# Mixed-head attention and two feed-forward blocks: the head mix ahead of the softmax as three float32r matmuls on rows split two steps ahead

## Chip, cores and metric

One core of a Trainium2 chip runs the whole program. The metric is the device time of one execution in microseconds; the kernel before has a median of 704.97 us over 3 runs (704.95 to 705.08).

## The reference, cut to what matters

```python
# q, k, v: (2, 12, 448, 64);  w_pre, w_post: (12, 12);  float32 throughout
scores = scale * (q @ k^T)                       # per batch and head, 448 x 448
scores = einsum('bhij,hg->bgij', scores, w_pre)  # mix of the heads ahead of the softmax
scores = scores - max(scores, axis=-1)
attn   = exp(scores)
attn   = attn / (sum(attn, axis=-1) + 1e-9)
attn   = einsum('bhij,hg->bgij', attn, w_post)   # mix of the heads behind it
x      = (attn @ v), heads side by side          # 896 x 768
x      = moe(x)    # h = x @ w_in (768 x 2048); h * clip(h + 3, 0, 6) / 6; @ w_out
out    = moe2(x)   # h = x @ w_in; max(h, 0) + alpha * min(h, 0); @ w_out
```

## The kernel before

**Tiles and groups.** The query rows of each batch are cut into tiles of 120 rows (120, 120, 120, 88), eight tiles in all. For each tile and head, TensorE (PE) computes the scores (`qk`, line 197), and ScalarE copies them from PSUM into a tile `S` that has one query row per partition (line 597). The mix runs over heads, so heads must lie on partitions: a DMA (`pull`, line 208) takes 10 query rows of all 12 heads, 120 partition rows of 448 numbers, into a tile `pull`. Such a unit is a group; there are 90 groups.

**Steps.** One loop over `s_` writes the order of the work out by hand; a step is one turn of it. Step `s_` mixes group `s_` with a block-diagonal 120x120 weight (`premix`, line 224: PE in float32, which the trace shows as two matmul records per group), and VectorE takes the negated row maximum (line 226). ScalarE computes the exponential with row sums (`exp`, line 234). In the next step `norm` adds 1e-9 to the sums, inverts them (lines 215, 216), and scales a copy `wr` of the post-mix weights by them (line 218), all on VectorE. Three steps behind `premix`, `post` (line 244) multiplies the exponentials with `wr` in float32 on PE (eight records), and ScalarE evicts the result into `MT` (line 257).

**Around it.** In the same step PE computes the scores of a coming tile, mostly one head (two float32r matmuls with query halves split into a rounded part and its rest); the queries' split is on GpSimd (POOL, lines 169 and 170). In steps 22 to 33 the keys of the second batch are split, one head per step: a cast on VectorE (line 153) and a subtraction on GpSimd (line 154). When all groups of a tile are post-mixed, `av` (line 281) multiplies `MT` with the values: six head pairs per tile, in two bursts of three pairs, half a tile's steps apart; VectorE copies the sums to `xT` (line 294). In steps 57 to 77 the first three weight blocks of the feed-forward part are loaded and converted from 64-bit storage (lines 346 to 369; ScalarE, VectorE, GpSimd in successive steps). From step 77 on there are no more scores to compute; `xT` is split (`split_x`, lines 441 and 442) and the blocks too (lines 374 and 380), and from step 84 on the first feed-forward matmuls (line 446) run between the groups. The feed-forward part that follows, from about 249 us on, is almost PE alone: three float32r matmuls per product (`mm3`).

**Queues and buffers.** Every engine works through its instructions in order. All DMAs are issued by SP. PSUM holds two buffers for the mixed scores (`mx`), two for the scores, two for `post`, two for `av`. `pull` runs four steps ahead and has six buffers.

Of the kernel before, what the change touches and what calls it, by code (L numbers as in the profile page):

```python
# [7 lines left out]
F32 = mybir.dt.float32  # L8
R = mybir.dt.float32r
# [4 lines left out]
ALU = mybir.AluOpType  # L14
# [2 lines left out]

LAG = 3
PL = 4
EB = 384  # L20

W_MIN = 2.0 ** -15
# [13 lines left out]
def kernel(  # L36
# [15 lines left out]
    nc = tc.nc  # L52
    _, D, H, S = k.shape
# [6 lines left out]
    GP = G * H  # L60
# [3 lines left out]
    tiles = []  # L64
    groups = []
    for b in range(B):
        for i0 in range(0, S, GP):
            n = min(GP, S - i0)
            t = len(tiles)
# [7 lines left out]
    NTILE, NG = len(tiles), len(groups)  # L77
# [9 lines left out]
    def pool(stack, name, **kw):  # L87
        return stack.enter_context(tc.tile_pool(name=name, reuse_waits="tile", **kw))
# [5 lines left out]
    late = pool(p_late, "late", bufs=3)  # L94
# [6 lines left out]
    with tc.manual_schedule():  # L101
# [5 lines left out]
        xT = xtp.tile([128, KD, NT], F32, name="xT")  # L107
# [94 lines left out]
        d_t, mx_t, e_t, sm_t, wr_t, pt_t = {}, {}, {}, {}, {}, {}  # L202

        def pull(g):
            ti, o, st, xn = groups[g]
            t = late.tile([GP, S], F32, tag="pull", bufs=PL + 2, name="pull")
            src = S_t[ti][bass.ds(o, xn, step=st)] if st > 1 else S_t[ti][o:o + xn]
# [4 lines left out]
        def norm(g):  # L212
            pm = groups[g][3] * H
            sm = sm_t.pop(g)[:pm]
            nc.vector.tensor_scalar(sm, sm, 1e-9, None, ALU.add)  # L215
            nc.vector.reciprocal(sm, sm)
            wr = wr_t[g] = late.tile([GP, GP], F32, tag="wr", bufs=LAG + 1, name="wr")
            nc.vector.tensor_scalar(wr[:pm], wpost[:pm], sm, None, ALU.mult)

        def premix(g):  # L220
            pn = groups[g][3] * H
            d = d_t.pop(g)
            m = psA.tile([GP, 512], F32, tag="mx", bufs=2, name="mx")
            nc.tensor.matmul(m[:pn, :S], wpre[:pn, :pn], d[:pn], start=True, stop=True)  # L224
            nm = late.tile([GP, 1], F32, tag="nm", name="nm")
            nc.vector.tensor_reduce(nm[:pn], m[:pn, :S], axis=AX.X, op=ALU.max, negate=True)  # L226
            mx_t[g] = (m, nm)
# [69 lines left out]
        qk_at, av_at = {}, {}  # L297
        for ti in range(1, NTILE):
            lo, hi = tiles[ti - 1]["s"] - PL, tiles[ti]["s"] - PL
            first = range(HC) if ti == 1 else ()  # L300
            for h in first:
                qk_at[lo + 1 + h] = [(ti, h)]
            for s_, hs in spread(list(range(len(first), H)), lo + (PL if first else 0), hi).items():
                qk_at.setdefault(s_, []).extend((ti, h) for h in hs)
        k_first = {
            tiles[ti - 2]["s"] - PL - 2: tiles[ti]["b"] for ti in range(tps, NTILE, tps)
        }
        for ti in range(NTILE - 1):
            lo = tiles[ti]["s"] + tiles[ti]["ng"] + LAG
            for z in range(2):  # L310
                av_at[lo + 2 + z * (tiles[ti + 1]["ng"] // 2)] = [(ti, 3 * z + a) for a in range(3)]


        P = {}
# [56 lines left out]
        def conv_hi(i):  # L371
            if i < len(blocks):
                hi = P["w"].tile([128, WC], R, tag="whi", bufs=3, name="whi")
                nc.scalar.copy(hi, b_t[i])  # L374
                w_t[i] = [hi]

        def conv_lo(i):
            if i < len(blocks):
                lo = P["w"].tile([128, WC], R, tag="wlo", bufs=3, name="wlo")
                nc.gpsimd.tensor_tensor(lo, b_t.pop(i), w_t[i][0].bitcast(F32), ALU.subtract)  # L380
                m = KD if blocks[i][0] == "in" else 2
                w_t[i] = [x.rearrange("p (k f) -> p k f", k=m) for x in (w_t[i][0], lo)]
# [56 lines left out]
        def split_x(kk, c, a, z, src, eng):  # L439
            h, l = x_pair(kk, c)  # L440
            nc.scalar.copy(h[:, a:z], src)
            eng.tensor_tensor(l[:, a:z], src, h[:, a:z].bitcast(F32), ALU.subtract)
# [83 lines left out]
            nc.sync.dma_start(out=wmix[nm], in_=src)  # L526
        load_q(1, 0)
        wpre = wmix["pre"]

        wpost = late.tile([GP, GP], F32, tag="wpost", bufs=1, name="wpost")  # L530
        for j in range(H // 2):
# [6 lines left out]
        nc.gpsimd.tensor_copy(  # L538
            wpost.rearrange("p (g x) -> p x g", g=H), wmix["post"].rearrange("p (x g) -> p x g", g=H)
        )  # L540
        for s_ in range(-PL, 6 - PL):
            for (ti, h) in qk_at.get(s_, []):
                if h % HC == 0 and h:
                    load_q(ti, h // HC)

        X = tiles[-1]["s"] - PL
        also = {}

        def at(s_, *fs):
            also.setdefault(s_, []).extend(fs)  # L550

        a = tiles[-3]["s"]
        for i in range(NC):
            at(a, lambda i=i: load_w(i))
            for z, f in enumerate((conv_magnitude, conv_shift, conv_sign, conv_round)):
                at(a + 3 + z, lambda f=f, i=i: f(i))
            a += 7
        at(X, open_early)
        at(X + 1, lambda: nc.sync.dma_start(out=alpha_sb, in_=alpha.rearrange("(k p) -> p k", p=128)))
        for kk in range(KD):  # L560
            at(X + 1 + kk, lambda kk=kk: split_x(kk, 0, 0, S, xT[:, kk, :S], nc.gpsimd))
        for i in range(NC):
            at(X + 2 + 3 * i, lambda i=i: conv_hi(i), lambda i=i: conv_lo(i))
        at(X + 7, lambda: load_w(3), lambda: load_w(4))
        at(NG, lambda: conv_a(3))
        at(NG + 1, lambda: conv_round(3))
# [7 lines left out]
        for s_ in range(-PL, NG + LAG):  # L574
            for g in range(PL) if s_ == -PL else [s_ + PL] if 0 <= s_ < NG - PL else []:
                pull(g)
            for c in range(2) if s_ in k_first else ():
                load_k(k_first[s_], c)
            for ti in range(tps, NTILE, tps):
                if s_ == tiles[ti]["s"] + tiles[ti]["ng"] + LAG:  # L580
                    for c in range(4):
                        load_v(tiles[ti]["b"], c)
            if 0 <= s_ < 4:
                load_v(0, s_)
            if s_ in range(NG):
                premix(s_)
            kk = s_ - (NG - KD)
            if kk == 0:
                p0 = ptile()[:, :S]
            if 0 <= kk < KD:  # L590
                in_part(p0, 0, x_t, 0, kk, kk + 1)
            heads = qk_at.get(s_, [])
            pend = [qk(ti, h, s_ < 0 and h % 2) for (ti, h) in heads]
            if s_ in range(NG):
                exp(s_)
            for z, (d, p) in enumerate(pend):
                (nc.vector.tensor_copy if s_ < -1 and z == 1 else nc.scalar.copy)(d, p)
            for (ti, h) in qk_at.get(s_ + 6, []):
                if h % HC == 0:
                    load_q(ti, h // HC)  # L600
            for (ti, h) in qk_at.get(s_ + 2, []):
                if h % HC == 0:
                    split_q(ti, h // HC)
            for (ti, h) in qk_at.get(s_ - 2, []):
                if ti % tps == tps - 1 and ti + 1 < NTILE:
                    split_k(tiles[ti + 1]["b"], h)
                    if h in (2, 5):
                        load_k(tiles[ti + 1]["b"], h // HC + 2)
            if s_ - 1 in range(NG):
                norm(s_ - 1)  # L610
            if s_ - LAG in range(NG):
                post(s_ - LAG)
                post_evac(s_ - LAG)
            if s_ == NG:
                p1 = in_chain(1, x_t, 0)
                gs[0, 0] = g_tile(0, 0)
                run(act1(p0, gs[0, 0], 0))
            if s_ == NG + 1:
                p2 = ptile()[:, :S]
                in_part(p2, 2, x_t, 0, 0, KD // 2)  # L620
            if s_ == NG + 2:
                in_part(p2, 2, x_t, 0, KD // 2, KD)
                gs[1, 0] = g_tile(1, 0)
                run(act1(p1, gs[1, 0], 1))
            for (ti, h) in av_at.get(s_, []):
                av(ti, h)
            for f in also.get(s_, []):
                f()
# [26 lines left out]
        def out_layer(i, gs, done):  # L655
            for e in range(DM // EB):
                accs = [ptile()[:, :S] for _ in range(2 * EB // 128)]
                for f2 in range(KF // 2):
# [8 lines left out]
                    wt = w_t.pop(i)  # L667
                    for ee in range(EB // 128):
                        for c in range(B):
# [6 lines left out]
                            if last:  # L676
                                done(e * (EB // 128) + ee, c, p)
                    i += 1
# [28 lines left out]
def _laid_out(q, k, v, w_pre, w_post, moe_w_in, moe_w_out, moe2_w_in, moe2_w_out, moe2_alpha):  # L707
# [26 lines left out]
    def w_out(w):  # L734
        f, m = w.shape
        w = w.view(_np.int64).reshape(f // 256, 2, 128, m // EB, EB)
        return w.transpose(3, 0, 2, 1, 4).reshape(-1, 128, 2 * EB)

# [36 lines left out]
```

## Time and profile before

| | |
|---|---|
| median of 3 runs | 704.97 us |
| the profiled execution | 705.02 us, its span 703.0 us, mean granted TensorE clock 0.995 |
| PE busy | 691.4 us (98%) |
| VectorE (DVE) busy | 440.5 us (63%) |
| ScalarE (ACT) busy | 372.5 us (53%) |
| GpSimd (POOL) busy | 324.4 us (46%) |
| chain that ended last | PE 89%, of it line 446 58%, line 244 11%, line 224 10%, line 281 6%, line 197 5% |

A page is of one profiled execution. Busy is the union of an engine's instructions; successive instructions of one engine can overlap by some hundredths to tenths of a microsecond, so what an instruction takes of its queue is the distance between starts. The chain of waits follows the work that ended last back to what released it.

### The profile page before, as it was taken

The numbers are of one execution on the slowest core, as the hardware profiler recorded it, in microseconds if no ns is written. First come the engines' busy times: TensorE is split into PE (matmuls) and PEld (weight loads), VectorE is DVE, ScalarE is ACT, GpSimd is POOL, SyncE is SP. The second block draws the span as 40 slices with busy tenths as digits, with TensorE's granted clock in tenths as the row PEclk, the third lists the DMA queues.
The fourth block names the chain that finished last, engine by engine and source line by source line (L and its number), as shares of the span: only waits on it lengthen the run. The fifth ranks groups of instructions, "written<-read, shape, count | busy, mean of one in ns | idle before, by whom it ended". The sixth has DMA issues, their size and how long they took to land.

```text
span 703.0 us, 11160 instructions
## 1 busy us (share of the span) xinstructions
PE 691.4 (98%) x4164; PEld 610.0 (87%) x4164; DVE 440.5 (63%) x778; ACT 372.5 (53%) x692; POOL 324.4 (46%) x224
## 2 busy tenths in 40 slices
PE   5999999999999999999999999999999999999998
PEld 2677778877788899999999999999999999999997
DVE  5565874456666458888874454348999999535311
ACT  4686566667776656656554443343444454444300
POOL 6331651212226235454567555544455455775630
PEclk9899999999999999999999999999999999999999
DMA  4755554346446022323334423322223322445302
GB/s 154 225 176 181 160 137 124 108 153 190 153 105 163 1 91 90 130 96 102 123 101 154 139 99 105 122 90 86 94 91 113 113 90 95 148 158 182 124 1 78
DMA packets 31874, 85.20 MB, mean 121 GB/s; under 512 B 5966, under 2 KB 21966, under 8 KB 31822
## 3 DMA queue, kind: packets, MB, share of 16 engines
q1 hardware_dynamic: 31822, 84.50, 37.2%
q8 instruction: 33, 0.54, 0.3%
q14 instruction: 19, 0.16, 0.1%
HBM read 62.47 MB, written 2.75 MB: 93 GB/s over the span
## 4 chain that ended last, share of the span: by engine, by line
PE 89%; POOL 6%; issue 3%; DMA 0%; SPq 0%; DVE 0%; POOLq 0%
PE p L446 58%; PE pt L244 11%; PE mx L224 10%; PE av L281 6%; PE sc L197 5%; POOL wb L369 2%; POOL wlo L380 2%; POOL kT L160 1%; DMA kst<-in_k_dram 0%; SPq L127 0%; POOL qT L170 0%; POOL qT L169 0%; POOL wmix_pre L536 0%; POOL wpost L538 0%; DVE o L694 0%
## 5 line engine op out<-in xcount | busy, mean ns | idle before, releaser
L380 POOL TENSOR_TENSOR wlo<-wb,whi 128x768 fp32r<-128x768 f32 x64 | 126.4, 1974 | 127.3 <-ACT whi L374 127.3
L369 POOL TENSOR_TENSOR wb<-wb,wst 128x768 int32<-128x768 int32 x64 | 125.5, 1962 | 101.3 <-DVE wb L362 79.0
L446 PE MATMUL p<-xh,whi 128*128 128x448 f32 x384 | 141.7, 369 | 0.0
L446 PE MATMUL p<-gl,whi 128*128 128x448 f32 x384 | 139.4, 363 | 0.0
L446 PE MATMUL p<-xl,whi 128*128 128x448 f32 x384 | 139.4, 363 | 0.0
L446 PE MATMUL p<-gh,whi 128*128 128x448 f32 x384 | 139.2, 362 | 0.0
L446 PE MATMUL p<-gh,wlo 128*128 128x448 f32 x384 | 138.4, 360 | 0.1
L446 PE MATMUL p<-xh,wlo 128*128 128x448 f32 x384 | 138.3, 360 | 0.0
L354 DVE TENSOR_SCALAR wb<-wb 128x768 f32<-128x768 f32 x64 | 52.6, 822 | 81.6 <-ACT wb L346 81.5
L346 ACT ACTIVATE wb<-wst 128x768 f32<-128x768 f32 x64 | 57.8, 904 | 68.9 <-DMA wst<-in_w_out_dram 50.1
L244 PEld LDWEIGHTS pt<-wr,e 120*112 120x112 f32 x720 | 86.8, 176 | 7.4 <-issue 2.3
L234 ACT ACTIVATE e<-mx,nm 120x448 f32<-120x448 f32 (+1 forms) x90 | 57.2, 635 | 63.2 <-DVE sm L215 46.5
L244 PE MATMUL pt<-wr,e 120*112 120x120 f32 x720 | 88.5, 266 | 0.0
L224 PE MATMUL mx<-pull,wmix_pre 120*120 120x448 f32 x180 | 85.7, 559 | 2.3 <-DMA pull<-S 2.3
L226 DVE TENSOR_REDUCE nm<-mx 120x1 f32<-120x448 f32 (+1 forms) x90 | 55.9, 621 | 45.1 <-PE mx L224 45.0
L374 ACT CAST whi<-wb 128x768 fp32r<-128x768 f32 x64 | 53.2, 832 | 50.6 <-PE p L446 32.4
L446 PEld LDWEIGHTS p<-xh,whi 128*128 128x128 f32 x384 | 72.1, 188 | 6.8 <-issue 1.2
L446 PEld LDWEIGHTS p<-gh,whi 128*128 128x128 f32 x384 | 72.1, 188 | 5.7
L446 PEld LDWEIGHTS p<-gh,wlo 128*128 128x128 f32 x384 | 71.8, 187 | 5.6 <-POOL wlo L380 0.5
L446 PEld LDWEIGHTS p<-xh,wlo 128*128 128x128 f32 x384 | 71.8, 187 | 5.1
L446 PEld LDWEIGHTS p<-xl,whi 128*128 128x128 f32 x384 | 72.1, 188 | 4.7 <-issue 0.9
L197 PE MATMUL sc<-kT,qT 128*120 128x448 f32 (+1 forms) x168 | 75.3, 535 | 0.4 <-POOL qT L170 0.3
(52 smaller groups left out, 896.7 us busy)
## 6 DMA issues: line engine op xcount, KB each, us to landing
wst<-in_w_in_dram SPq DMA_DIRECT2D x32, 768.0 KB
wst<-in_w_out_dram SPq DMA_DIRECT2D x32, 768.0 KB
pull<-S SPq DMA_DIRECT2D x88, 210.0 KB
qst<-in_q_dram SPq DMA_DIRECT2D x20, 180.0 KB
kst<-in_k_dram SPq DMA_DIRECT2D x5, 672.0 KB
v<-in_v_dram SPq DMA_DIRECT2D x8, 336.0 KB
out_dram<-o SPq DMA_DIRECT2D x12, 224.0 KB
qst<-in_q_dram SPq DMA_DIRECT2D x8, 132.0 KB
```

What stands on the lines that cost most here:

```text
L197: nc.tensor.matmul(p[:n, :S], t[:, o, a:a + n], kT[h], start=(o == 0), stop=(o == 1))
L224: nc.tensor.matmul(m[:pn, :S], wpre[:pn, :pn], d[:pn], start=True, stop=True)
L226: nc.vector.tensor_reduce(nm[:pn], m[:pn, :S], axis=AX.X, op=ALU.max, negate=True)
L234: nc.scalar.activation(out=e[:pn], in_=m[:pn, :S], func=ACTF.Exp, bias=nm[:pn], accum_out=sm[:pn])
L244: nc.tensor.matmul(p[:, c * GP:(c + 1) * GP], e[:pn, c * JP:(c + 1) * JP], wr[:pn], start=True, stop=True,)
L281: nc.tensor.matmul(p[64 * o:64 * o + 64, a % 3, :n], v_t[T["b"], h // HC][:, h % HC, c, :], MT[ti][:, c, h, :n], start=(c == 0), stop=(c = ...
L346: nc.scalar.activation(t, s[:, :, 1].bitcast(F32), ACTF.Abs)
L354: nc.vector.tensor_scalar(t, t, W_MAX, W_MIN, ALU.min, ALU.max)
L369: nc.gpsimd.tensor_tensor(n, n, st_t.pop(i)[:, :, 0].bitcast(I32), ALU.add)
L374: nc.scalar.copy(hi, b_t[i])
L380: nc.gpsimd.tensor_tensor(lo, b_t.pop(i), w_t[i][0].bitcast(F32), ALU.subtract)
L446: nc.tensor.matmul(p, wt[a], xt[c], start=(first and z == 0), stop=(last and z == 2))
```

## The change

Groups 0 and 1 are mixed as before. For every later group, two steps ahead of the mix, the pulled rows are rounded to float32r (`sh`; on ScalarE for odd groups, on VectorE for even ones, with some exceptions near the weight conversion), and VectorE subtracts the rounded rows from the pulled ones in place. The mixing weights are split in the same way once. The mix is then three matmuls: rounded weights with rounded rows, rounded weights with the rest, rest of the weights with rounded rows.

`norm` moves from behind the score work to right behind the maximum, and its scaling goes to GpSimd, except in steps with a weight conversion on GpSimd. All six pairs of `av` come in one burst per tile. The second batch's value loads are spread over four steps, and a few splits of activations and weights change their steps.

```diff
+RAW = 2
@@ norm
-            nc.vector.tensor_scalar(wr[:pm], wpost[:pm], sm, None, ALU.mult)
+            if g in by_vector:
+                nc.vector.tensor_scalar(wr[:pm], wpost[:pm], sm, None, ALU.mult)
+            else:
+                nc.gpsimd.tensor_scalar(wr[:pm], wpost[:pm], sm, 1.0, ALU.mult, ALU.mult)
+
+        def split_s(g):
+            if RAW <= g < NG:
+                pn = groups[g][3] * H
+                d = d_t.pop(g)
+                t = late.tile([GP, S], R, tag="sh", bufs=2, name="sh")
+                (nc.scalar.copy if g in by_scalar else nc.vector.tensor_copy)(t[:pn], d[:pn])
+                r = d.bitcast(R)
+                nc.vector.tensor_tensor(r[:pn], d[:pn], t[:pn].bitcast(F32), ALU.subtract)
+                d_t[g] = (t, r)
@@ premix
-            nc.tensor.matmul(m[:pn, :S], wpre[:pn, :pn], d[:pn], start=True, stop=True)
+            if g < RAW:
+                nc.tensor.matmul(m[:pn, :S], wpre[:pn, :pn], d[:pn], start=True, stop=True)
+            else:
+                for z, (a, x) in enumerate(((0, 0), (0, 1), (1, 0))):
+                    nc.tensor.matmul(
+                        m[:pn, :S], wpre_r[a][:pn, :pn], d[x][:pn], start=(z == 0), stop=(z == 2)
+                    )
@@ value bursts
-            for z in range(2):
-                av_at[lo + 2 + z * (tiles[ti + 1]["ng"] // 2)] = [(ti, 3 * z + a) for a in range(3)]
+            av_at[lo + 2] = [(ti, a) for a in range(H // 2)]
@@ start
+        wpre_r = [late.tile([GP, GP], R, tag=f"wpre{z}", bufs=1, name=f"wpre{z}") for z in "hl"]
...
+        nc.gpsimd.tensor_scalar(wpre_r[0], wpre, 1.0, 1.0, ALU.mult, ALU.mult)
+        nc.gpsimd.tensor_tensor(wpre_r[1], wpre, wpre_r[0].bitcast(F32), ALU.subtract)
@@ who does what in the steps with a weight conversion (a = 57, 64, 71)
+        by_vector = set()
+        by_scalar = set(range(1, NG, 2))
...
+            by_vector |= {a + 6, a + 7}
+            by_scalar -= {a + 5}
+            by_scalar |= {a + 7}
@@ splits of activations and weights
-            at(X + 1 + kk, lambda kk=kk: split_x(kk, 0, 0, S, xT[:, kk, :S], nc.gpsimd))
+            at(X + 1 + kk + (kk > 1), lambda kk=kk: split_x(kk, 0, 0, S, xT[:, kk, :S], nc.gpsimd))
-            at(X + 2 + 3 * i, lambda i=i: conv_hi(i), lambda i=i: conv_lo(i))
+            at(X + (3, 8, 10)[i], lambda i=i: conv_hi(i), lambda i=i: conv_lo(i))
@@ the loop over steps
-                if s_ == tiles[ti]["s"] + tiles[ti]["ng"] + LAG:
-                    for c in range(4):
+                if tiles[ti]["s"] + LAG + 4 <= s_ < tiles[ti]["s"] + LAG + 8:
+                    for c in (s_ - tiles[ti]["s"] - LAG - 4,):
                         load_v(tiles[ti]["b"], c)
...
             if s_ in range(NG):
                 premix(s_)
+            if s_ - 1 in range(NG):
+                norm(s_ - 1)
+            if s_ in range(NG):
+                split_s(s_ + 2)
...
-            if s_ - 1 in range(NG):
-                norm(s_ - 1)
             if s_ - LAG in range(NG):
                 post(s_ - LAG)
```

## Rows read from the trace of the kernel before

**Rows 1.** Busy time of each engine, its share of the span, instructions.

```profile
PE 691.4 (98%) x4164; PEld 610.0 (87%) x4164; DVE 440.5 (63%) x778; ACT 372.5 (53%) x692; POOL 324.4 (46%) x224
```

**Rows 2.** Chain of waits in order of time: start us, us, what.

```profile
146.74 0.75 PE mx L224 x2
147.49 0.41 PE sc L197 x2
147.90 0.82 PE pt L244 x8
...
196.13 2.61 PE av L281 x48
198.75 0.94 PE mx L224 x2
...
240.72 1.81 PE p L446 x9
```

**Rows 3.** Timeline of ScalarE: start, us, engine, line, operation, out<-in [idle before].

```profile
144.28 0.63 ACT L234 ACTIVATE e<-mx,nm 120x448 f32<-120x448 f32 x1 [0.37 <-DVE sm L215]
...
144.90 0.52 ACT L597 COPY S<-sc 120x448 f32<-120x448 f32 x1
145.31 0.59 ACT L257 COPY MT<-pt 112x480 f32<-112x480 f32 x1
```

**Rows 4.** Timeline of VectorE, the same step.

```profile
143.56 0.62 DVE L226 TENSOR_REDUCE nm<-mx 120x1 f32<-120x448 f32 x1 [0.79 <-PE mx L224]
144.10 0.14 DVE L215 TENSOR_SCALAR sm<-sm 120x1 f32<-120x1 f32 x1
144.28 0.17 DVE L216 RECIPROCAL sm<-sm 120x1 f32<-120x1 f32 x1
144.48 0.28 DVE L218 TENSOR_SCALAR wr<-wpost,sm 120x120 f32<-120x120 f32 x1
```

**Rows 5.** Lines 153 and 488: duration ns min/median/max, first and last start us.

```profile
L153 DVE CAST kT<-kst x12: 376/377/926, 66.8 to 94.7; 128x448 fp32r<-128x448 f32 x12
...
L488 DVE TENSOR_TENSOR gl<-t,gh x32: 612/618/1920, 474.7 to 593.6; 128x448 fp32r<-128x448 f32 x32
```

**Rows 6.** Groups by form: count, busy us, mean ns of one, idle before.

```profile
L154 POOL TENSOR_TENSOR kT<-kst,kT 64x448 fp32r<-64x448 f32 x12 | 13.7, 1139 | 22.5 <-DVE sm L215 19.9 <-PE pt L244 2.1 <-issue 0.4
L169 POOL TENSOR_SCALAR qT<-qst 128x360 fp32r<-128x360 f32 x19 | 9.7, 511 | 60.5 <-DMA qst<-in_q_dram 48.0 <-PE sc L197 10.1 <-PE pt L244 2.2
L442 POOL TENSOR_TENSOR xl<-xT,xh 128x448 fp32r<-128x448 f32 x6 | 6.8, 1140 | 4.6 <-ACT xh L441 4.6
L170 POOL TENSOR_TENSOR qT<-qst,qT 128x264 fp32r<-128x264 f32 x8 | 6.2, 773 | 0.7
L441 ACT CAST xh<-xT 128x448 fp32r<-128x448 f32 x6 | 3.5, 582 | 0.0
L536 POOL TENSOR_SCALAR wmix_pre<-wmix_pre 120x120 f32<-120x120 f32 x1 | 0.7, 725 | 0.1
```

**Rows 7.** Timeline of VectorE around step 87.

```profile
222.85 1.59 DVE L218 TENSOR_SCALAR wr<-wpost,sm 120x120 f32<-120x120 f32 x1
```

**Rows 8.** Timeline of GpSimd, the same stretch.

```profile
222.55 1.82 POOL L380 TENSOR_TENSOR wlo<-wb,whi 128x768 fp32r<-128x768 f32 x1 [1.66 <-ACT whi L374]
```

**Rows 9.** Stretches: us, busy PE, PEld, DVE, ACT, POOL, clock, DMA share, GB/s.

```profile
65.34:95.41 30.07, 30.07 (x244) 23.30 (x243) 25.66 (x61) 19.82 (x50) 18.05 (x19) 1.00 0.50 160
162.63:200.75 38.12, 38.12 (x326) 30.20 (x325) 24.12 (x70) 28.46 (x67) 7.11 (x8) 1.00 0.49 160
202.74:220.97 18.23, 18.23 (x146) 14.35 (x145) 14.32 (x40) 15.18 (x37) 12.14 (x9) 1.00 0.59 125
```

**Rows 10.** Timeline at the start of the steps, PE.

```profile
17.05 1.48 PE L224 MATMUL mx<-pull,wmix_pre 120*120 120x448 f32 x2 [2.31 <-DMA pull<-S]
...
18.62 0.28 PEld L197 LDWEIGHTS sc<-kT,qT 128*120 128x120 f32 x1 [1.31 <-POOL qT L169]
```

## The prediction

> **What bounds the kernel now.** I read the page's busy shares first, then the chain of waits in order of time, then single steps on the timeline. PE is busy 691.4 of 703.0 us [rows 1]. In the chain a step of the attention stage is PE alone, end to end: mixing pair 0.75 us, two score matmuls 0.41, eight post matmuls 0.82, sum 1.98, and the next step begins where it ends [rows 2]. So what PE sheds is gained, as long as the others deliver in that time. ScalarE has 0.37 us left per step: the score copy starts 0.62 behind the exponential, the eviction 0.41 behind the copy and takes 0.59, of which some 0.1 overlaps what follows: 1.5 together [rows 3]. VectorE uses about 1.1: maximum, the add and the reciprocal take the queue 0.54, 0.18 and 0.20, so 0.92, then the scaling of the post weights [rows 4]. The change spends these reserves.
>
> **PE.** Nine float32r matmuls of 448 columns took 1.81 us on the chain [rows 2], 0.20 each, three 0.60. Against 0.75 that is 0.15 us per group, and 88 of the 90 groups change: 13.2 us. A step would take 1.83. The first mixing pair behind a value burst took 0.94 instead of 0.75 [rows 2]; 14 half bursts become 7 whole ones, 7 x 0.19 = 1.3 us. If nothing else moved, 705.0 - 14.5 = 690.5.
>
> **What VectorE pays.** Every group adds a subtraction with two SBUF inputs: 0.62 us, 0.54 of the queue (as for the maximum, which overlaps its successor by 0.08). Even groups add a rounding copy, 0.38 by the nearest row [rows 5]; odd ones give it to ScalarE, 0.58 by the nearest row [rows 6], about 0.47 of its queue, so 0.24 per step on the mean: 1.74 of 1.83. The scaling of the weights leaves VectorE for GpSimd. Its price there: a tensor_scalar of 360 columns took 0.51, the one of the same 120x120 shape 0.73 beside a working VectorE [rows 6]; between a third of the first (0.17) and 0.73, I take 0.27, since 0.73 holds a wait.
> The two engines stand in each other's way here: while GpSimd's 1.82 us subtraction ran from 222.55 on, a VectorE tensor_scalar that takes 0.28 [rows 4] took 1.59 [rows 7] and ended when that did [rows 8]. The copy ranged from 0.38 to 0.93 and the two-input subtraction from 0.61 to 1.92 [rows 5]. Reductions from PSUM show no such stretch.
> So in a regular step, from maximum to maximum: odd 0.92 + 0.54 = 1.46; even 0.92 + 0.38 + 0.04 (dependent start) + 0.25 (the weights' scaling slips in on GpSimd between copy and subtraction) + 0.54 = 2.13; mean 1.80. A query split on GpSimd (0.51 + 0.77 us, some every third step [rows 6]) can hold VectorE between 0 and 0.4 per step; it mostly runs beside the maximum, so I take 0.1: 1.9 against PE's 1.83. The whole burst of 5.2 us per tile (twice 2.61 [rows 2]) lets VectorE catch up the 0.8 that it falls behind in 12 steps. So 55 regular steps (10 to 21, 34 to 76) keep their saving: 55 x 0.15 = 8.3 us.
>
> **Where the reserve is gone.** Four places.
> - Steps 59 to 75, with the early weight conversion: VectorE was busy 24.12 of 38.12 us [rows 9], 1.42 per step. Plus 0.54, plus half a copy 0.17, minus the scaling 0.20, plus 0.15 of waiting: 2.08 x 17 = 35.4, against PE's new 35.6. No slack, and the conversion comes in lumps: I charge 1.5 us (bounds 0 and 2.6, their whole saving).
> - Steps 22 to 33 split the next batch's keys: per step a VectorE cast and a GpSimd subtraction of 1.14 us [rows 6]; these steps took 30.07 us with two half bursts [rows 9]. The GpSimd subtraction starts some 0.15 behind the cast and holds VectorE's next copy or subtraction until 1.29, though the statistics are done at 0.84. Odd: 1.29 + 0.48 + 0.25 (scaling on GpSimd) + 0.26 (cast) = 2.3. Even: 1.29 + 0.26 + 0.25 + 0.48 + 0.30 = 2.6. Four query splits add 1.2 each, 0.4 per step: 2.85 x 12 = 34.2 us; 1.3 of this is carried out as VectorE's lag into steps with a little reserve: 32.9, so 2.8 us are lost against before (bounds: 1.8 gained if the engines interleave, 6 lost if all waits add).
> - Steps 77 to 85 have no score matmuls, PE 1.57 before; 18.23 us with a half burst [rows 9], 15.4 without. GpSimd has six activation subtractions of 1.14 [rows 6], three weight passes of 1.82 [rows 8] and seven scalings: 14.2 us; VectorE's copies, subtractions and two scalings hold the same path for 9 x 0.54 + 4 x 0.30 + 2 x 0.2 = 6.5. One after the other 20.7, so 5.3 more; the burst at step 86 hides two VectorE steps of lag, 3.3: 2.0 lost (bounds: 1.3 gained, 5 lost). Steps 86 to 89 gain 4 x 0.15 = 0.6.
> - The start: GpSimd splits the mixing weights ahead of a query split for which PE waited 1.31 us [rows 10]: two operations on 120 columns, 0.5 to 1.5 us. Against it stand the 8 x 0.15 = 1.2 of steps 2 to 9. I take zero for both (bounds 0.7 gained, 1.5 lost).
>
> The moves cost nothing by themselves. Adding and inverting the sums behind the maximum delays no exponential (ScalarE already waits for the maximum alone); the value loads are spread over four steps, before the burst that reads them, so SP's pulls wait less. The split waits for a pull two steps earlier than the mixing did; behind a waiting copy on ScalarE stands that step's exponential, behind VectorE's subtraction the next maximum. One pull held PE, the first, for 2.31 us [rows 10]; later ones never did. Taken at nothing, upper bound in the rivals.
>
> **Sum.** 8.3 - 1.5 - 2.8 - 2.0 + 0.6 + 1.3 + 0 = 3.9 us. The profiled execution took 705.02 (span 703.0 and 2.0 around it), the median 704.97, so they are one number here: 705.0 - 3.9 = 701.1 us.
>
> **Rivals.**
> 1. PE stays the only bound: VectorE and GpSimd interleave, buffers carry the lag. For it: VectorE's idle time of 0.79 us per step before its maximum [rows 4] and the bursts. Against it: 2.1 us in an even step. Time: 690.5 plus about 1 at the start, 691.5.
> 2. Slower: the path that VectorE and GpSimd share becomes the step. Place: the copy or subtraction behind the reciprocal. Price: the scaling (0.27) in odd steps too and 0.3 of query split per step: (1.46 + 0.27 + 2.13) / 2 + 0.3 = 2.2 us; less the burst's help, two steps' lag, some 0.2 per step: 2.0, PE's old step. The regular saving of 8.3 is then nil, the losses stay: 705.0 + 1.5 + 2.8 + 2.0 - 1.3 = 710.0 us. It decides from 1.98 us from maximum to maximum on. The stretched scaling of 1.59 us speaks for it, the long quiet stretches of GpSimd against it (7.11 of 38.12 us busy [rows 9]). The Trainium skill ("Perfetto Trace Analysis", section Optimizing Scalar/DVE Operations) speaks against the change in this sense: the two engines share an SBUF read port, so that moving work between them might not help. By that rule the scaling on GpSimd frees nothing, which is this rival's 710; the stretched 1.59 us [rows 7] agrees that one waits for the other.
> 3. Pulls land too late for the earlier split. At seven tile starts the pulls wait for the last score copy; half a us to a us each, 3.5 in sum: 701.1 + 3.5 = 704.6, no change. For it the 2.31 us at the start; against it that no other pull was waited for.
> 4. The three matmuls don't cost less than the pair (0.25 each, 0.75 in all): then 710.0 as well. Against it the score pair, two float32r matmuls in 0.41.
>
> **Chances.** Forecast 0.45, with a range of its own of 698 to 704; rival 1 0.20; rival 2 0.20; rival 3 0.12; rival 4 0.03. The range of 692 to 708.5 leaves out the fast half of rival 1 and the worse half of rivals 2 and 4. A measurement of this kernel tells about 0.2%, 1.4 us, from no change. Faster than 703.6: 0.42 of the forecast, all of rival 1, a little of rival 3: 0.63. Within: 0.11. Slower than 706.4: rivals 2 and 4 and what is worse of 3: 0.26.
>
> **What would show it.** The timeline of PE: three mixing matmuls 0.20 apart and a step of 1.83 us around 145 us; if they are 0.25 apart, rival 4. VectorE's distance from maximum to maximum, odd against even: 1.5 and 2.1, below 1.83 on the mean; from 1.98, rival 2. Steps 22 to 33 and 77 to 85: their windows longer than before, with PE idle ahead of the mixing matmuls; if they are shorter, rival 1. Waits of ScalarE's or VectorE's split for a pull: rival 3. One burst of 5.2 us per tile. The feed-forward stage behind about 249 us must keep its length to 0.5 us; if it doesn't, the reasoning left something out. Wrong altogether: a gain above 14.5 us, or a loss in the regular steps.

## The result and the profile after

The changed kernel takes 715.0 us (713.76 to 716.19, 4 runs) against 705.03, ratio 1.0142, 95% interval 1.013 to 1.0154: 10 us slower, where 701.1 was forecast. Its profiled execution took 714.41 us, span 712.6.

Busy shares and the chain by line, from the page of the changed kernel; the first line answers to [rows 1]:

```profile
PE 686.7 (96%) x4252; PEld 625.5 (88%) x4252; DVE 486.5 (68%) x825; ACT 392.2 (55%) x737; POOL 378.7 (53%) x310
...
PE 75%; DVE 8%; POOL 7%; issue 4%; DMA 4%; ACT 1%; SPq 0%; POOLq 0%; ACTq 0%
PE p L465 57%; PE av L301 5%; PE pt L264 5%; PE mx L242 4%; DMA pull<-S 4%; DVE pull L231 3%; PE sc L198 3%; POOL wb L388 2%; DVE nm L246 2%; POOL wlo L399 2%; POOL kT L161 1%; DVE sh L229 1%; DVE kT L154 1%; DMA kst<-in_k_dram 0%; ACT e L254 0%
```

PE is busy 4.7 us less and yet ends 10 us later: the chain, 89% PE before, now has only 75% on PE and leads over VectorE (8%) and over DMA (4%, the pulls) too. The PE part did what it should. Chain of waits in order of time, a regular stretch (start us, us, what), against [rows 2]:

```profile
127.59 0.61 PE mx L242 x3
128.21 0.41 PE sc L198 x2
128.62 0.82 PE pt L264 x8
129.44 0.61 PE mx L242 x3
```

Three mixing matmuls take 0.61 us instead of 0.75, and the step is 1.85 instead of 1.98. VectorE keeps up there (timeline of VectorE, an odd step, against [rows 4], and the next two maxima):

```profile
130.09 0.62 DVE L246 TENSOR_REDUCE nm<-mx 120x1 f32<-120x448 f32 x1
130.63 0.14 DVE L216 TENSOR_SCALAR sm<-sm 96x1 f32<-96x1 f32 x1
130.80 0.16 DVE L217 RECIPROCAL sm<-sm 96x1 f32<-96x1 f32 x1
131.06 0.63 DVE L231 TENSOR_TENSOR pull<-pull,sh 120x448 fp32r<-120x448 f32 x1
131.92 0.62 DVE L246 TENSOR_REDUCE nm<-mx 120x1 f32<-120x448 f32 x1 [0.24 <-PE mx L242]
...
134.28 0.61 DVE L246 TENSOR_REDUCE nm<-mx 120x1 f32<-120x448 f32 x1
...
135.61 0.62 DVE L246 TENSOR_REDUCE nm<-mx 120x1 f32<-120x448 f32 x1
```

It still waits 0.24 us for PE at the end of it. The even step behind takes 2.36 us from maximum to maximum, the next odd one 1.33: 1.85 on the mean. Where it goes wrong is seen by stretches. The table has the time between the starts of the row maximum of two steps, read from the timelines (us); the work of the value bursts is the same in each row but the last, in which the changed kernel, e4 and e6 have another half burst of 2.6.

```
steps    before  after    e1     e4     e6     e8    e10    e11    e12
0-9       19.1   20.0   20.0   20.5   21.1   18.9   17.7   19.7   19.6
9-24      35.4   33.8   33.3   33.3   33.8   33.3   33.2   33.3   33.3
24-36     30.6   34.7   35.0   30.1   34.7   30.8   29.8   33.9   33.3
36-47     27.8   26.9   26.4   26.7   26.8   26.5   26.3   26.5   26.4
47-57     24.2   23.6   22.8   23.3   22.3   22.8   22.8   22.8   22.8
57-69     30.0   33.4   30.0   33.8   31.0   29.7   28.5   29.2   30.0
69-81     27.2   30.5   29.6   30.5   30.5   27.2   26.0   26.3   31.9
81-89     18.4   21.5   18.3   21.5   21.5   18.4   18.6   18.3   18.2
```

Gains stand in steps 9 to 24 and 36 to 57, losses in 24 to 36 (+4.2), 57 to 69 (+3.4) and 69 to 81 (+3.3). Each column is one profiled execution. The first row moves by more than a microsecond between runs with the same code there and carries no conclusion; the row 69 to 81 is 29.6 in e1 and 31.9 in e12 with the same code (the clock, at the end of the next section).

Two windows of the changed kernel, steps 22 to 33 and 77 to 85 (columns as in [rows 9], whose first and third row they answer to):

```profile
67.30:100.76 33.46, 29.81 (x257) 25.43 (x256) 28.10 (x65) 22.36 (x55) 25.01 (x32) 1.00 0.49 152
...
211.10:230.51 19.41, 16.53 (x108) 13.67 (x107) 18.62 (x43) 16.34 (x40) 14.99 (x14) 1.00 0.58 123
```

PE idles 3.7 and 2.9 us in them; before it was busy throughout. The granted clock stays at 1.00 (2.4 GHz). In the second VectorE is busy 18.62 of 19.41 us.

**VectorE and GpSimd hold each other up.** Timeline of VectorE, steps 24 and 25, and below it of GpSimd:

```profile
73.44 0.92 DVE L229 CAST sh<-pull 120x448 fp32r<-120x448 f32 x1
74.39 0.67 DVE L231 TENSOR_TENSOR pull<-pull,sh 120x448 fp32r<-120x448 f32 x1
74.98 0.59 DVE L154 CAST kT<-kst 128x448 fp32r<-128x448 f32 x1
75.50 0.60 DVE L246 TENSOR_REDUCE nm<-mx 120x1 f32<-120x448 f32 x1
...
76.28 1.61 DVE L231 TENSOR_TENSOR pull<-pull,sh 120x448 fp32r<-120x448 f32 x1
77.81 0.38 DVE L154 CAST kT<-kst 128x448 fp32r<-128x448 f32 x1
78.11 0.61 DVE L246 TENSOR_REDUCE nm<-mx 120x1 f32<-120x448 f32 x1
```

```profile
72.96 1.15 POOL L155 TENSOR_TENSOR kT<-kst,kT 64x448 fp32r<-64x448 f32 x1
...
76.27 1.14 POOL L155 TENSOR_TENSOR kT<-kst,kT 64x448 fp32r<-64x448 f32 x1
77.50 0.84 POOL L222 TENSOR_SCALAR wr<-wpost,sm 120x120 f32<-120x120 f32 x1
```

In the first step the rounding copy, 0.38 us where nothing holds it, lasts 0.92, until GpSimd's subtraction begun at 72.96 has ended plus 0.25; in the second the subtraction, 0.62 alone, lasts 1.61, until the GpSimd subtraction begun at 76.27 has ended, at 77.41, plus 0.48. GpSimd waits in its turn: the scaling at 77.50 lasts 0.84. The row maximum, which reads PSUM, is not stretched (0.61 at 78.11, beside that scaling). VectorE's step is 2.6 us here.

**The pulls.** Timeline of SP, then of ScalarE, then of VectorE, steps 52 to 58:

```profile
149.74 0.48 SPq L135 DMA_DIRECT2D v<-in_v_dram  x1
...
151.71 0.48 SPq L135 DMA_DIRECT2D v<-in_v_dram  x1
152.29 0.82 SPq L209 DMA_DIRECT2D pull<-S  x1
153.17 0.67 SPq L135 DMA_DIRECT2D v<-in_v_dram  x1
153.94 0.93 SPq L209 DMA_DIRECT2D pull<-S  x1
```

```profile
159.78 0.56 ACT L229 CAST sh<-pull 120x448 fp32r<-120x448 f32 x1 [2.81 <-DMA pull<-S]
160.25 0.63 ACT L254 ACTIVATE e<-mx,nm 120x448 f32<-120x448 f32 x1
```

```profile
156.88 0.39 DVE L229 CAST sh<-pull 120x448 fp32r<-120x448 f32 x1 [1.37 <-DMA pull<-S]
...
157.85 0.62 DVE L246 TENSOR_REDUCE nm<-mx 120x1 f32<-120x448 f32 x1
```

The pulls of the new tile stand among value loads of 336 KB. The copies wait 1.37 and 2.81 us for them, and behind each stands what the running step needs: the maximum, the exponential. The maxima of steps 57 and 58 come 3.2 and 3.3 us behind the ones before them. The view of waits sums it up for the whole stage (us in total, times, longest):

```profile
ACT sh L229 <- DMA pull<-S: 7.2, 4, 2.8
...
DVE sh L229 <- DMA pull<-S: 4.2, 5, 1.4
```

### The profile page after: what moved, and what is told of

It reads as the page before. It is cut to its first block, busy times and chain, and to the rows that moved or that the text cites. A ratio compares the mean times of both kernels' runs of the same rounds, so it can differ in the third digit from the quotient of the medians.

```text
span 712.6 us, 11559 instructions
## 1 busy us (share of the span) xinstructions
PE 686.7 (96%) x4252; PEld 625.5 (88%) x4252; DVE 486.5 (68%) x825; ACT 392.2 (55%) x737; POOL 378.7 (53%) x310
## 4 chain that ended last, share of the span: by engine, by line
PE 75%; DVE 8%; POOL 7%; issue 4%; DMA 4%; ACT 1%; SPq 0%; POOLq 0%; ACTq 0%
PE p L465 57%; PE av L301 5%; PE pt L264 5%; PE mx L242 4%; DMA pull<-S 4%; DVE pull L231 3%; PE sc L198 3%; POOL wb L388 2%; DVE nm L246 2%; POOL wlo L399 2%; POOL kT L161 1%; DVE sh L229 1%; DVE kT L154 1%; DMA kst<-in_k_dram 0%; ACT e L254 0%
## 5 line engine op out<-in xcount | busy, mean ns | idle before, releaser
L465 PE MATMUL p<-xh,whi 128*128 128x448 f32 x384 | 139.6, 363 | 0.0
L222 POOL TENSOR_SCALAR wr<-wpost,sm 120x120 f32<-120x120 f32 (+1 forms) x84 | 47.6, 566 | 88.9 <-DVE sm L217 64.1
L254 ACT ACTIVATE e<-mx,nm 120x448 f32<-120x448 f32 (+1 forms) x90 | 57.6, 640 | 38.4 <-DVE sm L216 29.6
L465 PEld LDWEIGHTS p<-gl,whi 128*128 128x128 f32 x384 | 72.1, 188 | 3.6
L231 DVE TENSOR_TENSOR pull<-pull,sh 120x448 fp32r<-120x448 f32 (+1 forms) x88 | 66.2, 752 | 8.7 <-ACT sh L229 5.7
```

The costliest lines, as they stand in the source:

```text
L222: nc.gpsimd.tensor_scalar(wr[:pm], wpost[:pm], sm, 1.0, ALU.mult, ALU.mult)
L231: nc.vector.tensor_tensor(r[:pn], d[:pn], t[:pn].bitcast(F32), ALU.subtract)
L254: nc.scalar.activation(out=e[:pn], in_=m[:pn, :S], func=ACTF.Exp, bias=nm[:pn], accum_out=sm[:pn])
L465: nc.tensor.matmul(p, wt[a], xt[c], start=(first and z == 0), stop=(last and z == 2))
```

## The experiments

Times are medians; before ran at 704.6 to 705.05 beside them. A diff is against the changed kernel unless it says otherwise.

**e1, value part back** (the value part: the whole bursts and the moved value loads).

```diff
-            av_at[lo + 2] = [(ti, a) for a in range(H // 2)]
+            for z in range(2):
+                av_at[lo + 2 + z * (tiles[ti + 1]["ng"] // 2)] = [(ti, 3 * z + a) for a in range(3)]
-                if tiles[ti]["s"] + LAG + 4 <= s_ < tiles[ti]["s"] + LAG + 8:
-                    for c in (s_ - tiles[ti]["s"] - LAG - 4,):
+                if s_ == tiles[ti]["s"] + tiles[ti]["ng"] + LAG:
+                    for c in range(4):
```

> The changed kernel with the value part put back: two half bursts per tile and the second batch's value loads all in step 60, as before. In the changed kernel's trace the pulls of groups 58 to 62 are issued beside those loads, the split copies of steps 57 and 58 waited 1.4 and 2.8 us for them, and these two steps took 3.2 and 3.3 us instead of 1.84. Theory pulls: these steps fall back to about 1.9, 3 to 4 us come back, and 1.3 are paid for seven more bursts: 712.5 us against 715.0. Rival, the path shared by VectorE and GpSimd explains everything: the loads don't matter, and the additional bursts cost 1.3: 716.3, or less if two catch-ups per tile help VectorE more than one.

708.51 us, ratio 1.0062 (1.004 to 1.0085): 6.5 us back, more than the theory asked. Steps 57 to 69 fall from 33.4 to 30.0. ScalarE's wait for pulls falls from 7.2 us to the one of 2.8 in step 27:

```profile
ACT sh L229 <- DMA pull<-S: 2.8, 1, 2.8
```

**e5 and e6, which half of it.** e5: `whole = ti == 3`, loads as changed; e6: `whole = ti != 3`, loads as before.

```diff
-            av_at[lo + 2] = [(ti, a) for a in range(H // 2)]
+            whole = ti == 3
+            for z in range(1 if whole else 2):
+                av_at[lo + 2 + z * (tiles[ti + 1]["ng"] // 2)] = [(ti, 3 * z + a) for a in range(6 if whole else 3)]
```

> The changed kernel with two half bursts per tile again, but for tile 3, whose burst stays whole so that the value loads can stay in steps 52 to 55. Putting back both gave 715.0 to 708.5 us. Theory loads: the collision of value loads and pulls is the larger part, it stays: 712 us, steps 57 to 69 still near 33. Rival bursts: a whole burst takes away one of two chances per tile at which VectorE catches up, and that is the larger part: 709.5 us, steps 57 to 69 near 30.5.

> The counterpart: whole bursts, but for tile 3, which has two halves, and the value loads all in step 60 as before. Theory loads: 711.5 us, steps 57 to 69 back from 33.4 to about 30.5. Rival bursts: 714 us or more, steps 69 to 89 as slow as in the changed kernel.

e5 714.53 us (1.0122 to 1.0153), e6 711.89 (1.0093 to 1.0127). So the loads' place is worth 6.0 us with half bursts (714.5 to 708.5) and 3.1 with whole ones (715.0 to 711.9); the bursts are worth 3.4 and 0.5. The loads are the larger part. How much is due to each stays rough: the four runs of e5 and of e6 spread over 2 us, those of e1 over 3.4, and some 1.6 us of e5's profiled execution are a fallen clock (end of this section); by that estimate the loads would be worth 4.4 with half bursts, the bursts 2.1 with the loads as changed.

**e9, the value part alone**, on the kernel before.

> The kernel before with only the value part: one whole burst per tile, the value loads in steps 52 to 55. Without the split nobody waits for a pull two steps ahead, and VectorE has 0.8 us idle per step. Theory: the value part is harmless by itself and hurts only beside the split; 7 x 0.19 us are gained as predicted, 703.6 us. Rival, the loads or the whole bursts cost by themselves: 706 us or more.

703.89 us, ratio 0.9992 (0.9982 to 1.0001). By itself the part does no harm; the 0.7 us gained can't be told from nothing. Beside the split, which needs the pulls two steps earlier, it does harm (e1).

**e2, scaling back on VectorE** (`if True:` for `if g in by_vector:`).

> The changed kernel with the scaling of the post-mix weights on VectorE in every step. Theory shared path: the scaling took 0.57 us on GpSimd on the mean (0.36 undisturbed) and held VectorE's copy or subtraction; on VectorE it costs 0.20 of the queue and waits where GpSimd works; in the regular steps VectorE stays within 1.84, in steps 22 to 35 it gains the scaling's 0.36 and pays 0.2: 713 us, 2 less. Rival, VectorE's own load is the bound: 0.2 more per step wherever VectorE sets the step (some 45 steps): 724 us.

718.37 us (1.0176 to 1.0207): 3.4 slower than with GpSimd. Neither number was right; the direction is the rival's. So the move to GpSimd helps, although the two engines hold each other up; that VectorE's own load is the reason is argued from the rival's condition.

**e3, no rest; e11, no rest and value part back.**

```diff
-                r = d.bitcast(R)
-                nc.vector.tensor_tensor(r[:pn], d[:pn], t[:pn].bitcast(F32), ALU.subtract)
-                d_t[g] = (t, r)
+                d_t[g] = (t, t)
```

> The changed kernel without the subtraction that makes the rest of the rows (the second matmul takes the rounded rows again, so the rest of the rows is left out of the result); copies, three matmuls and all else as they are. Theory VectorE and the shared path: 0.54 us and more per step are gone from VectorE, the copies remain; steps 22 to 35 and 59 to 87 come down to nearly PE's pace, 8 to 12 us less: 704 us, and the waits for pulls stay (4 us above rival 1 of the prediction and the start's 1.2). Rival, the pulls' landing sets the time: the copies wait as before, 712 or more.

> The changed kernel with the value part put back and without the subtraction for the rest of the rows (left out of the result: the second matmul takes the rounded rows again). Theory, two causes that add: 708.5 minus the 7.1 us that the subtraction was worth, 701.4 us, and below the kernel before. Rival, the two causes are one (VectorE's lag made the pulls late): 705 us or more.

e3 707.92 us (1.0032 to 1.0065), 7.1 less than the changed kernel; e11 704.33 (0.9979 to 1.001), 4.2 less than e1. The subtraction on VectorE costs 4 to 7 us as measured, and the two causes add only in part. Against expectation e11 keeps 33.9 us in steps 24 to 36: even without the subtraction 3.3 us are lost there against before. A late pull and the fallen clock behind it (end of this section) have them. Chain of waits of e11 there (start us, us, what):

```profile
75.37 0.62 DVE nm L244
...
76.33 5.10 DMA pull<-S
...
82.00 0.73 ACT e L252 x2
```

**e4, no key rest** (the line `nc.gpsimd.tensor_tensor(t[D:], src[D:], t[D:].bitcast(F32), ALU.subtract)` of the key split left out).

> The changed kernel without GpSimd's subtraction in the key split of steps 22 to 33 (12 x 1.14 us; the keys' rest is left out of the result). Theory shared path: steps 22 to 35, now 39.2 us, fall by the 4.5 us that they lost against before and by what of their 0.15 per step was kept back: 5 to 6 us less, 709.5 us. Rival, VectorE's own queue (0.92 + 0.54 + cast and copy, 1.9 per step) sets these steps: at most 1.5 less, 713.5.

709.96 us (1.0062 to 1.0092), 5.0 less; steps 24 to 36 at 30.1, 4.6 less than in the changed kernel and below before. The edit takes away both ways in which this subtraction can delay a step: that VectorE waits for it, and that a key load waits for it; e12 is about the second.

**e12, key loads later**, on e1: SP's key loads two steps later.

```diff
-                    if h in (2, 5):
-                        load_k(tiles[ti + 1]["b"], h // HC + 2)
+            for (ti, h) in qk_at.get(s_ - 4, []):
+                if ti % tps == tps - 1 and ti + 1 < NTILE and h in (2, 5):
+                    load_k(tiles[ti + 1]["b"], h // HC + 2)
```

> The changed kernel with the value part put back (708.5 us) and, besides, SP's two key loads of steps 24 and 27 issued two steps later. On SP the pull of group 29 stands behind the first of them, which waits until GpSimd has finished a key subtraction; the pull was issued at 76.75 us, its copy on ScalarE waited 2.8 us for it, and step 27 took 3.96 instead of some 2.6. Theory: the pulls of groups 29 and 30 go first, the wait is gone, and of the 4.5 us that steps 24 to 36 lose some 1.4 come back: 707.1 us, the rest of the loss there being the shared path. Rival, all of the loss is the late pull: 704.5. Other rival, VectorE's lag takes up what is freed: 708.5 unchanged.

707.56 us (1.0021 to 1.005). Its wait for the pull is gone and steps 24 to 36 fall by 1.7 to 33.3; the median's 0.9 is within the spread of either (706.7 to 709.4). In the changed kernel, e1 and e11 GpSimd's subtraction reached the exponential by way of SP: it held a key load, the load held the pull, the pull the copy. In the changed kernel the subtraction begun at 76.27 ends at 77.41 (shown above); SP and ScalarE go on:

```profile
77.43 0.34 SPq L113 DMA_DIRECT2D kst<-in_k_dram  x1
77.87 1.68 SPq L209 DMA_DIRECT2D pull<-S  x2
...
83.09 0.56 ACT L229 CAST sh<-pull 120x448 fp32r<-120x448 f32 x1 [2.66 <-DMA pull<-S]
```

The other 2.7 us of the stretch (33.3 in e12 against 30.6 before) are put down to VectorE waiting for GpSimd. No run shows that by itself; it agrees with e4, whose 4.6 less the 1.7 by way of SP leave 2.9.

**e7, the norm alone**, on the kernel before: `norm` behind the maximum, scaling on GpSimd.

> The kernel before with only the sums' inversion moved behind the maximum and the scaling on GpSimd; pair of float32 matmuls, bursts and loads as before. Theory: PE sets the step and VectorE gains room, no change, 705.0 us within 0.7. Rival, the scaling on GpSimd stretches steps 22 to 35 and 77 to 87, where GpSimd has other work: 707 us.

705.39 us, ratio 1.0012 (1.0002 to 1.0021): no gain, and at most 0.2% slower.

**e10, the matmuls alone**, on the kernel before: three matmuls from group 10 on, `d[:pn].bitcast(R)` three times, no split.

> The kernel before with three float32r matmuls from group 10 on, all three on the pulled rows as they are (the split of the rows is left out, and with it the result's accuracy and the rest of the rows); scaling, bursts and loads as before. Theory: PE alone decides here, 80 x 0.15 = 12 us less, 693 us: the matmuls' term of the prediction is right, and all that the change loses comes from the split and the moves. Rival, the three matmuls don't pay what two chain numbers promised, or ScalarE and DMA become the bound: 698 us or more.

696.12 us, ratio 0.9877 (0.9862 to 0.9891): 8.4 us of the 12. Steps 9 to 24 give 2.1 of 2.2 (14 or 15 groups at 0.15), 36 to 57 2.9 of 3.2; steps 24 to 36 0.7 of 1.8, and 81 to 89 none of 1.2. There other engines stood close behind PE even before, in the first VectorE with 25.66 of 30.07 us [rows 9].

**e8, the split where there is room**, on the kernel before, the rest of the change left out but for `norm` and the scaling of these groups.

```diff
+        split_on = set(range(10, 24)) | set(range(36, 60))
...
+            split_s(s_ + 2)
...
+        at(4, split_wpre)
```

> The kernel before with the split and the three matmuls only for groups 10 to 23 and 36 to 59, where neither keys are split nor weights converted nor activations split; scaling on GpSimd for these groups alone, the mixing weights split in step 4 instead of at the start; bursts and loads as before. Theory: the change pays where VectorE and GpSimd have room and costs elsewhere; the kernel with the value part put back gained 2.0, 1.4 and 1.3 us in steps 9 to 24, 36 to 47 and 47 to 57: 705.0 - 4.7 = 700.3 us. Rival, what VectorE falls behind there is only paid later, in the steps that follow: 703.5 or more.

699.61 us, ratio 0.9937 (0.9917 to 0.9957): 5.2 us faster than before, 15.4 faster than the changed kernel, within 0.7 of what was expected. The lag is not paid for later: steps 57 to 89 stand as before.

**The clock in these traces.** In e3, e11, e5, e12 and e2 the granted clock falls from 1.00 (2.4 GHz) to about 0.5 (1.2 GHz) for some us between 28 and 250 us, each time behind a stretch in which PE waited: in e12 PE was busy 2.19 of the 4.00 us from 208.00 on, in e11 0.26 of the 2.70 from 80.00 on. With nearly the same idle time (2.18 of 4.00 from 208.40 on) e1 keeps its clock. Windows of e12, e1 and e11 behind these stretches (columns as in [rows 9]):

```profile
212.00:214.00 2.00, 2.00 (x16) 1.78 (x16) 1.93 (x6) 2.00 (x6) 1.10 (x1) 0.50 0.61 135
...
212.40:214.40 2.00, 2.00 (x39) 1.98 (x40) 1.93 (x6) 2.00 (x6) 1.11 (x1) 1.00 0.59 132
...
84.00:87.00 3.00, 3.00 (x25) 2.78 (x25) 1.36 (x4) 3.00 (x9) 2.65 (x3) 0.51 0.87 319
```

In e11 the eight post matmuls take 1.67 us there instead of 0.98, the half burst 3.61 instead of 2.68: 1.6 us in sum, half of what steps 24 to 36 lose in it. In e5 and e12 it is again some 1.6 us, in steps 69 to 81 (31.2 in e5, 31.9 in e12, 29.6 in e1, the same code). So where PE waits, the change can pay a second time; without the fall, the subtraction would be worth some 6 us in e11 and 9 in e3, an estimate from one execution each. The changed kernel, e1 and e6 show no such fall.

## Why the prediction was wrong

The step that failed is the value part: "The moves cost nothing by themselves ... the value loads are spread over four steps, before the burst that reads them, so SP's pulls wait less", the earlier wait for the pulls "Taken at nothing", and 1.3 us gained by the bursts. e1 shows that this part costs 6.5 us in the changed kernel: with the 1.3, 7.8 of the 13.9 us between 701.1 and 715.0. The moved loads had been held against the burst that reads them, not against the pulls of the next tile, which the same change needed two steps earlier; and the half bursts' 0.19 us was counted, but not what two pauses per tile are worth against one when VectorE has little room (3.4 us by the medians with the loads out of the way, e6 against e1). That VectorE catches up in these pauses is not shown: by the table the two differ by 0.4 to 1.0 us in most rows, less than rows with the same code can differ.

The other 6.1 us stand in e1 already: 708.5, where the forecast without its bursts is 702.4. By the table two terms were mis-sized. For steps 57 to 76 a gain was forecast (20 x 0.15, less 1.5 for the conversion); e1 gains nothing in 57 to 69 and loses 1.0 in 69 to 77, 2.5 in all. And the key split's steps 24 to 36 lose 4.4 where 2.8 were charged. In steps 69 to 77 (before, e1, e11; one half burst in each; columns as in [rows 9]) it is the subtraction that fills VectorE:

```profile
185.62:203.88 18.26, 18.26 (x144) 14.18 (x144) 13.02 (x38) 14.02 (x34) 2.97 (x3) 1.00 0.34 115
...
186.32:205.56 19.24, 18.62 (x157) 16.11 (x156) 17.09 (x43) 16.34 (x39) 9.70 (x11) 1.00 0.31 109
...
184.00:201.40 17.40, 17.05 (x150) 15.19 (x149) 12.98 (x36) 15.58 (x38) 7.59 (x11) 1.00 0.38 123
```

VectorE is busy 17.09 of 19.24 us in e1; without the subtraction (e11) 12.98, and the steps fall below before.

Term by term:
- **PE, 0.15 us per group.** Right: 0.61 for 0.75. The sum of 13.2 us was not: e10 got 8.4 of 12.
- **Regular steps.** Right where no conversion runs: VectorE stays below PE's step, and rival 2's mark, 1.98 us from maximum to maximum, did not come. In steps 69 to 77 it did: (19.24 - 2.61) / 8 = 2.08 in e1, where before has (18.26 - 2.61) / 8 = 1.96. 8.3 us were counted for steps 10 to 21 and 34 to 76; e1, without the load collision, has 2.0 + 1.4 + 1.3 in steps 9 to 24 and 36 to 57, e8 5.2 in all.
- **Scaling on GpSimd.** 0.27 taken, 0.57 measured on the mean, 0.36 at least (line 222 of the changed kernel: min/median/max ns, first and last start):

```profile
L222 POOL TENSOR_SCALAR wr<-wpost,sm x84: 364/505/1395, 24.5 to 246.4; 120x120 f32<-120x120 f32 x82, 96x120 f32<-96x120 f32 x2
```

- **Steps 22 to 33.** Mechanism right, 2.8 us lost by the sum and 3.4 by the windows (33.46 against 30.07; one whole burst against two halves). By the table 4.2 in 24 to 36; e12 gives 1.7 of it to the late pull, for which no term stood.
- **Steps 59 to 75.** 1.5 us charged, 2.6 as the bound. 57 to 69 lost 3.4: with the loads alone put back they take 31.0 (e6), with the bursts too 30.0 (e1), as before; so 2.4 are the loads. 69 to 81 lost 3.3, and still 2.4 in e1; without the subtraction 26.3 (e11), below before.
- **Steps 77 to 85.** By the sum 5.3 lost up to the burst at step 86 and 3.3 hidden by it, so 2.0. Measured, without a half burst, from 18.23 less 2.8 to 19.41: 4.0 up to the burst. From step 77 to 89 it is 27.4 before and 30.3 after, 2.9 lost; the burst and the steps behind it gave back 1.1, not 3.3 and 0.6.
- **Start.** Zero taken. PE's load for the first scores now waits 1.77 us for the query split instead of 1.31 [rows 10], at 19.45 instead of 18.62: 0.8 of the bounds' 1.5 (timeline of PE in the changed kernel):

```profile
19.45 0.28 PEld L198 LDWEIGHTS sc<-kT,qT 128*120 128x120 f32 x1 [1.77 <-POOL qT L170]
```

- **Feed-forward stage.** From the maximum of step 89 to the end it is 471.7 us before, with a half burst of 2.6, and 469.4 after: its length is kept, as forecast.
- **Rival 3** had the mechanism, a copy in front of the exponential waiting for a pull, but placed it at the tile starts for the last score copy and priced it at 3.5 us with the rest of the sum kept. What made pulls late were value loads and a key load on SP. The waits for pulls are 11.4 us in sum, not all on the chain.
- The rule weighed beside **rival 2** (the Trainium skill, "Perfetto Trace Analysis", Optimizing Scalar/DVE Operations: moving work between engines that share a port might not help) is not borne out as a forecast here: with the scaling back on VectorE, e2 is 3.4 us slower. That one of the two waits for the other is borne out, by the copy of 0.92 and the subtraction of 1.61 us. The measurement decides: the scaling was better placed on GpSimd, and it is the subtraction on VectorE that costs (e3, e11).

## What to carry to other kernels

When work on an in-order engine begins to wait for a DMA earlier than before, go through SP's queue for every transfer in front of that DMA and beside it, the ones that the same change moves first; the slack that the old lead gave is not seen in any wait of the old profile. Loads that do no harm in their new place without the change (e9) can do harm with it (e1). A gain on the bounding engine that is paid for with elementwise work belongs only into the steps where the paying engines have room and do not hold each other up: with the value part put back the split lost 3.5 us over all groups (e1) and won 5.2 in 38 of the 90 (e8). Before counting a per-step saving over all steps, take the work away in an experiment or look step by step for a second engine that is already at the limit.

## What the runs showed of the hardware that was not expected

A GpSimd tensor_scalar with a per-row scalar on 120 columns takes 0.36 us at the least (line 222), where 360 columns with constants took 0.51 on the mean [rows 6]: a third of the columns, over two thirds of the time. GpSimd and VectorE hold each other up in both directions, in the timelines read here until the other's instruction has ended: VectorE's subtraction of 1.61 us ends 0.48 us behind GpSimd's, and GpSimd's scaling grew to as much as 1.40 us. A wait of PE can cost more than its length: behind waits like those of e11 and e12 the granted clock was about 0.5, which cost some 1.6 us more each time, and behind a like wait in e1 it was 1.00.
